# The first two token tiles of a feed-forward layer take their 16 hidden blocks in two alternating halves

## The chip, the cores and the metric

The kernel runs on one core of one Trainium2 chip. The metric is the device time of one execution in microseconds (us), the median of several runs. Beside it stands one profiled execution, from which all durations below come. Engines: PE is TensorE (matmul), DVE is VectorE, ACT is ScalarE, POOL is GpSimd, SP is SyncE, which here only issues DMAs.

## The reference, cut to what matters

A linear recurrence (state space attention) over 4 sequences of 768 steps with 8 heads is followed by a feed-forward layer over all 3072 tokens:

```python
# recurrence, chunk by chunk, for batch 4, heads 8, S = 768, D = 32, N = 16
L = np.exp(cum[:, :, :, None] - cum[:, :, None, :]) * causal
y_intra = np.einsum('bhij,bhjd->bhid', (Cc @ Bc.T) * L, xc)
y_inter = np.einsum('bhin,bhnd->bhid', Cc, state) * decay_to_i
state = decay_full * state + sum_j(Bc[j] * xc[j] * decay_from_j)
y[:, :, sl] = y_intra + y_inter
...
x = y.transpose(0, 2, 1, 3).reshape(3072, 256)
h = x @ w_in                       # w_in  [256, 2048]
g = softplus(h)
out = g @ w_out                    # w_out [2048, 256]
```

`w_in` and `w_out` arrive as float64. Every product of the feed-forward layer is done as three float32r matmuls of high and low parts, so the weights, the recurrence's output and the hidden values are all split in a high and a low part on the chip.

## The kernel before, in words

**Units and tiles.** The recurrence goes by 24 units of 128 tokens (`un0` to `un23`; 6 units to a sequence). The feed-forward layer goes by 6 token tiles of 512 tokens (`sizes`), so tile j needs units 4j to 4j+3. The hidden width of 2048 is cut into 16 blocks of 128 (`NFT`). A step (j, k) is block k of tile j.

**A step.** `first(j, k)` makes the hidden block `hp` in one of six PSUM banks (tag `ps`) by 6 matmuls of 512 columns: `xh*wih`, `xl*wih`, `xh*wil` for two halves of the contraction. ACT then makes the softplus `e` (3 buffers) and its rounded copy `gh` (4 buffers), and DVE the rest `gl = e - gh` (L531). `second(j, k)` adds the block to the two accumulators `acc0` and `acc1` by 6 more matmuls; each accumulator has one PSUM bank (pool `pa`). `second` of step s is written LAG = 8 steps after `first` of step s. When the last block of a tile is added, `finish(j)` copies `acc0` by DVE and `acc1` by ACT and sends both out.

**A unit.** Its rows arrive in `un` (3 buffers). POOL makes the decay mask `rm` (2 buffers), PE the scores `sp`, DVE the masked scores `m` (two instructions), PE the state update `zp` and the output `yp`, DVE the new `state` and the output `y`; ACT rounds `y` into the tile's `xh`, and POOL or DVE makes `xl = y - xh` (DVE for units 2, 4 and 7). Units from 8 on also need two DVE instructions on their raw B and C rows (`b_rows`, `c_all`, L199), and `c_all` is copied by DMA into `c_rows`, of which there is one. The first four units are written out by hand in the word list `ORDER`.

**The weights.** Sixteen loads `wraw0` to `wraw15` (even numbers: 2 blocks of `w_in`; odd: 2 blocks of `w_out`) each go through ACT (L475), three DVE instructions (L477, L479, L481), ACT (L484, the high part) and POOL or DVE (L486, the low part).

**What sets the order.** From step 0 on the program is written step by step: each step's `first`, softplus and split, the `second` of eight steps earlier, and then what is planned in that step: a unit's parts (`LATE`, `V_LAG`), loads, and one weight split a step in the order `W_ORDER`. A scheduler then puts each engine's instructions in one fixed order by its own estimate of times; on the chip each engine works its list in order, and an instruction that waits holds up all behind it on that engine.

Of the kernel before, what the change touches and what calls it, by code (L numbers as in the profile page):

```python
# [10 lines left out]
F32 = mybir.dt.float32  # L11
F32R = mybir.dt.float32r
I32 = mybir.dt.int32
BF16 = mybir.dt.bfloat16
AF = mybir.ActivationFunctionType
ALU = mybir.AluOpType
PSUM = bass.MemoryType.PSUM

P = 128
# [7 lines left out]
NFT = DFF // P  # L27
TOK = NB * S
HEAD = 4
# [22 lines left out]
ORDER = """  # L52
# [2 lines left out]
C3 I1 G0 G1 S3 warm1 R2 gg4 M2 W2 I2 R3 warm1 W0 X1 zero M3 w6 W2 I3 W2 G3 W2 X0 w4 X3 G2 w3 un5 X2  # L55
H0 H1
"""
W_ORDER = (0, 1, 4, 3, 2, 6, 10, 8, 5, 7, 12, 9, 14, 11, 13, 15)
LAG = 8
LATE = (1, 1, 1, 1, -1, -2, -1, -1)  # L60
V_LAG = (0, 0, 1, 0, 0, 2, 0, 0)

V_BP = (0, 2, 7)
V_CC = (0, 1, 2, 6, 7)
# [32 lines left out]
def recurrence_then_ffn(ctx: ExitStack, tc: tile.TileContext, fst, un, at, al, w_in, w_out, const, outT):  # L97
# [6 lines left out]
    p3 = ctx.enter_context(tc.tile_pool(name="p3", bufs=3))  # L104
# [17 lines left out]
    V, A, Pl, PE = (InOrder(e) for e in (nc.vector, nc.scalar, nc.gpsimd, nc.tensor))  # L122
# [3 lines left out]
    def load(out, in_):  # L126

        tc.keep_in_program_order(nc.sync.dma_start(out, in_))  # L128
# [143 lines left out]
    sizes = [512] * 6  # L272
    starts = [sum(sizes[:j]) for j in range(len(sizes))]
    xparts = {}

    def x_parts(t0):
        j = max(i for i in range(len(sizes)) if starts[i] <= t0)
        if j not in xparts:
            xparts[j] = [p3.tile([P, 2, 512], F32R, tag=f"x{v}", name=f"x{v}_{j}", bufs=2) for v in "hl"]
        return xparts[j], t0 - starts[j]  # L280

    bd = kb[:, 0 : NH // 2]
# [132 lines left out]
    def grow(i):  # L415
        y = mid[i]["y"] = p2.tile([P, 2, P], F32, tag="y", name=f"y{i}")
        V.tensor_tensor(y, mid[i]["yp"][:, : 2 * P].rearrange("p (g t) -> p g t", g=2), gg_s[i], op=ALU.mult)
        (xh, xl), c0 = x_parts(i * P)
        A.copy(xh[:, :, c0 : c0 + P], y)  # L419

    def rest(i):
        (xh, xl), c0 = x_parts(i * P)
        hi = xh[:, :, c0 : c0 + P].bitcast(F32)
        (V if i in V_XL else Pl).tensor_tensor(xl[:, :, c0 : c0 + P], mid.pop(i)["y"], hi, op=ALU.subtract)  # L424
# [19 lines left out]
    raws = {}  # L444

    def load_w(step):
        raw = p3.tile([P, 512, 2], I32, tag="wraw", name=f"wraw{step}", bufs=6)
        q = step // 2
        if step % 2 == 0:
            load(  # L450
                raw.rearrange("p (c f) t -> p c (f t)", c=2),
                w_in.rearrange("(c p) f -> p c f", p=P)[:, :, 512 * q : 512 * q + 512],
            )
        else:
            load(
                raw.rearrange("p (k e) t -> p k (e t)", k=2),
                w_out.rearrange("(k p) e -> p k e", p=P)[:, 2 * q : 2 * q + 2, :],
            )
        raws[step] = raw
# [33 lines left out]
    accs, parts = {}, {}  # L493
# [3 lines left out]
    def products(j, k, h, c0, c1):  # L497
        xh, xl = x_parts(starts[j])[0]
        fs = slice(k * P, (k + 1) * P)
        i = 0  # L500
        for c in range(2):
            for w, x in ((wih, xh), (wih, xl), (wil, xh)):
                PE.matmul(h[:, c0:c1], w[:, c, fs], x[:, c, c0:c1], start=i == 0, stop=i == 5)  # L503
                i += 1
# [28 lines left out]

    def second(j, k):
        n = sizes[j]
        if k == 0:
            accs[j] = [pa.tile([P, 512], F32, tag=f"acc{e}", name=f"acc{e}_{j}") for e in range(2)]
        acc = accs[j]
        gh, gl = parts.pop((j, k))
        for e in range(2):  # L540
            es = slice(e * P, (e + 1) * P)
            for i, (w, g) in enumerate(((woh, gh), (woh, gl), (wol, gh))):
                PE.matmul(  # L543
                    acc[e][:, :n], w[:, k, es], g, start=k == 0 and i == 0, stop=k == NFT - 1 and i == 2
                )

    def finish(j):
        t0, n = starts[j], sizes[j]
        for e in range(2):
            o = p2.tile([P, 512], F32, tag=f"o{e}", name=f"o{e}_{j}", bufs=1)  # L550
            if e == 0:
                V.tensor_copy(o[:, :n], accs[j][e][:, :n])  # L552
            else:
                A.copy(o[:, :n], accs[j][e][:, :n])
            load(outT[e * P : (e + 1) * P, t0 : t0 + n], o[:, :n])
# [22 lines left out]
    stages = defaultdict(list)  # L578
# [6 lines left out]
    def both(f, i):  # L585
# [11 lines left out]
        "un": load_unit,  # L597
        "gg": load_growth,
        "w": load_w,
        "loga": lambda _: log_clipped(la),  # L600
        "logr": lambda _: log_clipped(lr),
# [18 lines left out]
    for word in ORDER.split():  # L620
        name = word.rstrip("0123456789")
        acts[name](int(word[len(name) :] or 0))
    steps = [(j, k) for j in range(len(sizes)) for k in range(NFT)]

    def values(s):
        if s >= LAG:
            j, k = steps[s - LAG]
            second(j, k)
            if k == NFT - 1:
                finish(j)  # L630

    in_order[0] = False

# [2 lines left out]
    def plan(s, f, *args):  # L636
        fills[s].append((f, args))

    for i in range(HEAD, NB * NU):
        s = (i - HEAD) * NFT // 4  # L640
        late, wait = (LATE[i - HEAD], V_LAG[i - HEAD]) if i - HEAD < len(LATE) else (0, 2)
        s += late
        plan(s, prepare, i)
        plan(s, attend_scores, i)
        plan(s + wait, attend_values, i)
        if i + 2 < NB * NU:
            plan(s + 1, prefetch, i + 2)
    loads = [w for w in W_ORDER if f"w{w}" not in ORDER.split()]
    splits = [w for w in W_ORDER if w not in stages]
    for s, w in enumerate(splits):  # L650
        plan(s, split_w, w)
    for s, w in enumerate(loads):
        plan(s, load_w, w)
    for s in range(len(steps) + LAG):
        if s < len(steps):
            first(*steps[s])
            soft_part(*steps[s])
            split_part(*steps[s])
        values(s)
        for f, args in fills[s]:  # L660
            f(*args)
# [50 lines left out]
```

## Time and profile before

| What | Value |
|---|---|
| Median of 3 runs | 356.2 us (354.79 to 357.56) |
| The profiled execution: its time | 354.56 us |
| Its span, first to last instruction | 352.6 us |
| Busy over the span: PE, DVE, ACT, POOL | 94%, 56%, 48%, 32% |
| DVE busy per 10 us, from 40 to 100 us | 9.97, 9.89, 7.83, 9.23, 10.00, 10.00 us |
| DVE busy per 10 us, from 110 to 150 us | 4.14, 5.94, 5.08, 5.87 us |
| Mean granted TensorE clock | 0.98 |

PE's busy share says little by itself, since matmuls overlap and the end of each is modelled. How fast PE really moves is read from the starts of its matmuls, or from the chain of waits, which counts six 512-column matmuls as 1.36 us. The feed-forward layer alone is 96 x 12 = 1152 of them.

### The profile page before, as it was taken

To read this page: it belongs to the slowest core of one execution; us is meant where nothing else is said; L and a number is where in the kernel's file an instruction comes from. 1 tells how busy PE (TensorE), PEld (TensorE's weight loads), DVE (VectorE), ACT (ScalarE), POOL (GpSimd) and SP (SyncE) were. 2 spreads that over 40 slices of the span, in tenths; PEclk is the share of its full clock that TensorE was granted. 3 is DMA by queue.
4 is the path that set the end of the run, shared out by engine and by line. 5 is a ranking of instruction groups with operands and counts; after the bars stand their busy time and mean duration, and the time that the engine had idled before them with its cause. 6 is when DMAs were issued, how large, how long until landed. Compare 5 with 4: busy or idle time off the path is not lost.

```text
span 352.6 us, 5070 instructions
## 1 busy us (share of the span) xinstructions
PE 332.8 (94%) x1882; PEld 252.0 (71%) x1882; DVE 196.0 (56%) x300; ACT 168.4 (48%) x297; POOL 114.0 (32%) x142
## 2 busy tenths in 40 slices
PE   6878985999999999999999999999999999999995
PEld 3533653567677877787877787787787788888884
DVE  1676999799984545553653553754363523132231
ACT  2311835584665535454644544645353534344450
POOL 6576943557631125323143322323512000000000
PEclk9689999899999999999999999999999999999999
DMA  7889745364210752141543222552303100001001
GB/s 203 222 196 335 252 136 187 120 257 144 51 70 8 214 152 91 30 135 48 162 121 109 65 82 71 140 161 93 91 30 89 31 2 0 0 23 40 0 2 59
DMA packets 22264, 37.23 MB, mean 106 GB/s; under 512 B 1632, under 2 KB 12896, under 8 KB 22240
## 3 DMA queue, kind: packets, MB, share of 16 engines
q1 hardware_dynamic: 22240, 36.91, 34.6%
q8 instruction: 15, 0.25, 0.3%
q14 instruction: 9, 0.07, 0.1%
HBM read 29.46 MB, written 3.24 MB: 93 GB/s over the span
## 4 chain that ended last, share of the span: by engine, by line
PE 76%; DMA 9%; DVE 8%; issue 2%; SPq 2%; ACT 1%; DVEq 0%; ACTq 0%
PE acc L543 33%; PE hp L503 32%; DMA wraw<-in_w_out 3%; DMA gg<-gd 3%; PE yp L407 3%; DVE w L479 2%; PE yp L393 2%; PE sp L339 2%; SPq L128 2%; DMA head_c<-in_fst 2%; DVE gl L531 1%; DMA c_rows<-c_all 1%; DVE w L477 1%; DVE w L481 1%; PE zp L364 1%
## 5 line engine op out<-in xcount | busy, mean ns | idle before, releaser
L531 DVE TENSOR_TENSOR gl<-e,gh 128x512 fp32r<-128x512 f32 x96 | 71.5, 746 | 83.0 <-ACT gh L530 82.3
L530 ACT CAST gh<-e 128x512 fp32r<-128x512 f32 x96 | 59.3, 620 | 65.2 <-PE acc L543 64.2
L503 PE MATMUL hp<-xh,wih 128*128 128x512 f32 (+1 forms) x192 | 77.2, 405 | 6.3 <-ACT wih L484 5.1
L523 ACT ACTIVATE e<-hp 128x512 f32<-128x512 f32 x96 | 56.6, 595 | 49.6 <-DVE gl L531 42.3
L543 PE MATMUL acc<-gl,woh 128*128 128x512 f32 x192 | 75.0, 390 | 0.0
L503 PE MATMUL hp<-xl,wih 128*128 128x512 f32 (+1 forms) x192 | 74.9, 391 | 0.0
L543 PE MATMUL acc<-gh,wol 128*128 128x512 f32 x192 | 74.9, 393 | 0.0
L503 PE MATMUL hp<-xh,wil 128*128 128x512 f32 (+1 forms) x192 | 74.3, 390 | 0.0
L543 PE MATMUL acc<-gh,woh 128*128 128x512 f32 x192 | 73.1, 392 | 0.2 <-DVE o L552 0.2
L503 PEld LDWEIGHTS hp<-xh,wih 128*128 128x128 f32 x192 | 36.1, 188 | 19.4 <-ACT wih L484 6.0
L292 POOL TENSOR_SCALAR_AFFINE_SELECT rm<-fc 128x1024 f32<-128x1024 f32 x20 | 32.1, 1605 | 47.8 <-DVE m L350 47.7
L543 PEld LDWEIGHTS acc<-gh,woh 128*128 128x128 f32 x192 | 36.0, 188 | 8.2 <-issue 0.8
L503 PEld LDWEIGHTS hp<-xh,wil 128*128 128x128 f32 x192 | 36.1, 188 | 8.0 <-issue 0.2
L543 PEld LDWEIGHTS acc<-gh,wol 128*128 128x128 f32 x192 | 36.0, 188 | 7.9 <-issue 0.2
L543 PEld LDWEIGHTS acc<-gl,woh 128*128 128x128 f32 x192 | 36.1, 188 | 7.5
L503 PEld LDWEIGHTS hp<-xl,wih 128*128 128x128 f32 x192 | 36.4, 189 | 6.5 <-issue 0.2
L350 DVE TENSOR_TENSOR m<-sp,rm 128x512 f32<-128x512 f32 x40 | 26.2, 684 | 14.0 <-PE sp L339 12.5
L199 DVE SCALAR_TENSOR_TENSOR c_all<-un,kb,c_all 128x512 fp32r<-128x512 f32 x16 | 17.3, 1084 | 10.4 <-ACT c_all L198 10.2
L424 POOL TENSOR_TENSOR xl<-y,xh 128x256 fp32r<-128x256 f32 x18 | 14.0, 780 | 25.8 <-ACT xh L419 25.2
L320 POOL TENSOR_TENSOR r_apart<-un,fr 64x128 f32<-64x128 f32 x32 | 17.1, 534 | 14.1 <-DMA un<-in_un 10.1
L307 POOL TENSOR_TENSOR bp<-un,ft 128x128 f32<-128x128 f32 x15 | 7.4, 491 | 42.1 <-DMA un<-in_un 23.7
L383 POOL TENSOR_TENSOR tb<-state,kb 128x128 f32<-128x128 f32 x16 | 11.9, 744 | 23.6 <-DVE state L375 23.0
(96 smaller groups left out, 306.5 us busy)
## 6 DMA issues: line engine op xcount, KB each, us to landing
un<-in_un SPq DMA_DIRECT2D x16, 768.0 KB, 4.5
wraw<-in_w_in SPq DMA_DIRECT2D x8, 512.0 KB, 7.8
wraw<-in_w_out SPq DMA_DIRECT2D x8, 512.0 KB
c_rows<-c_all SPq DMA_DIRECT2D x32, 128.0 KB, 2.4
gg<-gd SPq DMA_DIRECT2D x16, 192.0 KB
out_t<-o SPq DMA_DIRECT2D x12, 256.0 KB
un<-in_fst SPq DMA_DIRECT2D x4, 576.0 KB, 9.6
head_c<-in_fst SPq DMA_DIRECT2D x8, 128.0 KB, 6.5
```

The lines of the kernel that those rows point to most:

```text
L199: V.scalar_tensor_tensor(out, raw, g, out.bitcast(F32), op0=ALU.mult, op1=ALU.add)
L292: Pl.affine_select(out=rm.rearrange("p h c i -> p (h c) i"), in_=fc[:, u].rearrange("p h c -> p (h c)").unsqueeze(2).broadcast_to([P, NH * ...
L320: (V if i in V_CC else Pl).tensor_tensor(cc[rows, g], un_s[i][rows, U_C:U_S].rearrange("p (c i) -> p c i", i=SUB), f_row[b][rows, u, :NC]. ...
L350: V.tensor_tensor(mid[i]["m"][:, 4 * g : 4 * g + 4].rearrange("p h t -> p (h t)"), mid[i].pop(("sp", g)), mid[i]["rm"][:, 4 * g : 4 * g + ...
L383: (V if i in V_TB else Pl).tensor_tensor(tb, state[i - 1].rearrange("p (e d) -> p e d", d=D).unsqueeze(1).broadcast_to([P, 2, 2, D]), bd.r ...
L407: PE.matmul(yp[32 * hh : 32 * hh + 32, g * P : (g + 1) * P], un_s[i][:, U_X + h * D : U_X + (h + 1) * D], m[:, h, :], start=u == 0, stop=u ...
L424: (V if i in V_XL else Pl).tensor_tensor(xl[:, :, c0 : c0 + P], mid.pop(i)["y"], hi, op=ALU.subtract)
L503: PE.matmul(h[:, c0:c1], w[:, c, fs], x[:, c, c0:c1], start=i == 0, stop=i == 5)
L523: A.activation(e, h, AF.Softplus)
L530: A.copy(gh, e)
L531: V.tensor_tensor(gl, e, gh.bitcast(F32), op=ALU.subtract)
L543: PE.matmul(acc[e][:, :n], w[:, k, es], g, start=k == 0 and i == 0, stop=k == NFT - 1 and i == 2)
```

## The change

Tiles 0 and 1 take their 16 blocks in halves, alternating: blocks 0 to 7 of tile 0, blocks 0 to 7 of tile 1, blocks 8 to 15 of tile 0, blocks 8 to 15 of tile 1. From tile 2 on the order is as before. After each first half ACT copies both accumulators into a buffer in SBUF (`keep_sums`, in a slot of the tag `wraw`), and `finish` of these two tiles adds it to the second half's sums by two DVE instructions. So the second eight blocks' weights are first used at step 16 in place of step 8, and tile 1's tokens at step 8 in place of step 16: units 4 to 7 are planned at steps 0, 1, 3 and 5 (before: 1, 5, 9 and 13), units 8 to 11 at 12, 16, 20, 24 (before: 15, 18, 23, 27), and the weight splits by the table `W_STEP` over steps 0 to 24, each loaded eight steps ahead. The raw weights get 5 buffers in place of 6, the tiles' inputs `xh`, `xl` 3 in place of 2.

```diff
-W_ORDER = (0, 1, 4, 3, 2, 6, 10, 8, 5, 7, 12, 9, 14, 11, 13, 15)
+W_ORDER = (0, 2, 4, 1, 6, 3, 5, 7, 8, 10, 12, 14, 9, 11, 13, 15)
+W_STEP = (0, 0, 0, 1, 3, 5, 7, 9, 11, 13, 15, 16, 18, 20, 22, 24)
 LAG = 8
-LATE = (1, 1, 1, 1, -1, -2, -1, -1)
-V_LAG = (0, 0, 1, 0, 0, 2, 0, 0)
+HALF = NFT // 2
+U_STEP = (0, 1, 3, 5, 12, 16, 20, 24)
+V_LAG = (0, 1, 1, 1, 0, 1, 0, 0)
...
-            xparts[j] = [p3.tile([P, 2, 512], F32R, tag=f"x{v}", name=f"x{v}_{j}", bufs=2) for v in "hl"]
+            xparts[j] = [p3.tile([P, 2, 512], F32R, tag=f"x{v}", name=f"x{v}_{j}", bufs=3) for v in "hl"]
...
-        raw = p3.tile([P, 512, 2], I32, tag="wraw", name=f"wraw{step}", bufs=6)
+        raw = p3.tile([P, 512, 2], I32, tag="wraw", name=f"wraw{step}", bufs=5)
...
     def second(j, k):
         n = sizes[j]
-        if k == 0:
+        if k % HALF == 0 and (k == 0 or j < 2):
             accs[j] = [pa.tile([P, 512], F32, tag=f"acc{e}", name=f"acc{e}_{j}") for e in range(2)]
...
+    def keep_sums(j):
+        both = p3.tile([P, 512, 2], I32, tag="wraw", name=f"half_{j}", bufs=5)
+        for e in range(2):
+            t = sums_of[j, e] = both.rearrange("p f t -> p (f t)").bitcast(F32)[:, 512 * e : 512 * e + 512]
+            A.copy(t, accs[j][e])
...
     def finish(j):
...
-            if e == 0:
+            if j < 2:
+                V.tensor_tensor(o, accs[j][e], sums_of[j, e], op=ALU.add)
+            elif e == 0:
...
-    steps = [(j, k) for j in range(len(sizes)) for k in range(NFT)]
+    steps = [(j, k) for v in range(2) for j in range(2) for k in range(v * HALF, v * HALF + HALF)]
+    steps += [(j, k) for j in range(2, len(sizes)) for k in range(NFT)]
...
             if k == NFT - 1:
                 finish(j)
+            elif k == HALF - 1 and j < 2:
+                keep_sums(j)
...
-        s = (i - HEAD) * NFT // 4
-        late, wait = (LATE[i - HEAD], V_LAG[i - HEAD]) if i - HEAD < len(LATE) else (0, 2)
-        s += late
+        s, wait = (U_STEP[i - HEAD], V_LAG[i - HEAD]) if i - HEAD < len(U_STEP) else ((i - HEAD) * NFT // 4, 2)
...
-    for s, w in enumerate(splits):
-        plan(s, split_w, w)
-    for s, w in enumerate(loads):
-        plan(s, load_w, w)
+    for s, w in zip(W_STEP, W_ORDER):
+        if w not in stages:
+            plan(s, split_w, w)
+        if f"w{w}" not in ORDER.split():
+            plan(max(s - 8, 0), load_w, w)
```

Line numbers of the changed kernel are 3 higher than before's in the parts named here (L484 for L481, and so on), and 18 higher at the end. In the rows below names read tile, unit or block, and a running number: `hp0_12_770` is the hidden block 12 of tile 0, `gl0_5_586` the low part of block 5 of tile 0, `y7_643` the output of unit 7, `xl_1_428` the low input of tile 1, `acc0_0_687` the first accumulator of tile 0.

On DVE, around the last unit of tile 1, before:

```order
L481 SCALAR_TENSOR_TENSOR w11_763<-wraw11_625,w11_763 128x512
L479 SCALAR_TENSOR_TENSOR w13_789<-wraw13_655,w13_789 128x512
L417 TENSOR_TENSOR y7_847<-yp7_837,gg6_476 128x256
L481 SCALAR_TENSOR_TENSOR w13_789<-wraw13_655,w13_789 128x512
L486 TENSOR_TENSOR wol_88<-w11_763,woh_87 128x512
L424 TENSOR_TENSOR xl_1_449<-y7_847,xh_1_448 128x2x128
```

and now:

```order
L489 TENSOR_TENSOR wol_88<-w7_716,woh_87 128x512
L420 TENSOR_TENSOR y7_643<-yp7_633,gg6_454 128x256
L534 TENSOR_TENSOR gl0_6_621<-e0_6_618,gh0_6_620 128x512
L480 TENSOR_SCALAR w10_860<-w10_860 128x512
L534 TENSOR_TENSOR gl0_7_662<-e0_7_659,gh0_7_661 128x512
L482 SCALAR_TENSOR_TENSOR w10_860<-wraw10_609,w10_860 128x512
L427 TENSOR_TENSOR xl_1_428<-y7_643,xh_1_427 128x2x128
```

Unit 7's output stood behind the three integer steps of fourteen weights and 12 of tile 0's `gl`; now it stands behind those of nine weights and 6 `gl`. Its low part `xl_1` is DVE's 53rd instruction after the second `m` of unit 4, where it was the 72nd.

On PE, where block 7 of tile 0 is added, before:

```order
L543 MATMUL acc0_0_640<-gh0_7_614,woh_87 128x512
L543 MATMUL acc0_0_640<-gl0_7_615,woh_87 128x512
L543 MATMUL acc0_0_640<-gh0_7_614,wol_88 128x512
L543 MATMUL acc1_0_641<-gh0_7_614,woh_87 128x512
L543 MATMUL acc1_0_641<-gl0_7_615,woh_87 128x512
L543 MATMUL acc1_0_641<-gh0_7_614,wol_88 128x512
L543 MATMUL acc0_0_640<-gh0_8_636,woh_87 128x512
```

and now:

```order
L506 MATMUL hp1_3_744<-xh_1_427,wih_85 128x512
L506 MATMUL hp1_4_770<-xh_1_427,wih_85 128x512
L342 MATMUL sp8_0_799<-c_rows_81,b_rows8_789 128x256 x2
L546 MATMUL acc0_0_687<-gl0_7_662,woh_87 128x512
L546 MATMUL acc0_0_687<-gh0_7_661,wol_88 128x512
L546 MATMUL acc1_0_688<-gl0_7_662,woh_87 128x512
L546 MATMUL acc1_0_688<-gh0_7_661,wol_88 128x512
L506 MATMUL hp1_0_674<-xl_1_428,wih_85 128x512
L506 MATMUL hp1_0_674<-xh_1_427,wil_86 128x512
```

Block 8 of tile 0 followed on block 7; now the products of tile 1 follow, of which the first matmul of each of five blocks stands ahead, and all the others behind the one that needs `xl_1`.

More of the change, by code (lines that the diff above doesn't have):

```diff
@@ L543, in second @@
                 PE.matmul(
-                    acc[e][:, :n], w[:, k, es], g, start=k == 0 and i == 0, stop=k == NFT - 1 and i == 2
-                )
+                    acc[e][:, :n],
+                    w[:, k, es],
+                    g,
+                    start=i == 0 and (k == 0 or k == HALF and j < 2),
+                    stop=i == 2 and (k == NFT - 1 or k == HALF - 1 and j < 2),
+                )
+    sums_of = {}
+    def keep_sums(j):
[3 more added lines that the diff above has]
+            A.copy(t, accs[j][e])
     def finish(j):
@@ L647, in recurrence_then_ffn @@
             plan(s + 1, prefetch, i + 2)
-    loads = [w for w in W_ORDER if f"w{w}" not in ORDER.split()]
-    splits = [w for w in W_ORDER if w not in stages]
-    for s, w in enumerate(splits):
-        plan(s, split_w, w)
-    for s, w in enumerate(loads):
-        plan(s, load_w, w)
+    for s, w in zip(W_STEP, W_ORDER):
[3 more added lines that the diff above has]
+            plan(max(s - 8, 0), load_w, w)
     for s in range(len(steps) + LAG):
```

## The prediction

> **What bounds the kernel now.** I read the page's slices first, then the chain of waits, PE's and DVE's rows in order of time, and last the counts of matmuls by stage.
>
> ```profile
> span 352.6 us, 5070 instructions
> PE   6878985999999999999999999999999999999995
> DVE  1676999799984545553653553754363523132231
> PEclk9689999899999999999999999999999999999999
> ```
>
> A slice is 8.8 us. DVE is full from the fifth slice to the eleventh and half idle afterwards, when PE is full: up to about 100 us DVE sets the pace, then PE. The last stops of PE, in its rows by time:
>
> ```profile
> 61.31 0.50 PE L503 MATMUL hp<-xh,wih 128*128 128x512 f32 x1 [3.74 <-ACT wih L484]
> 90.31 0.67 PE L393 MATMUL yp<-r_apart,tb 128*128 128x256 f32 x2 [0.84 <-DVE y L417]
> 113.66 0.47 PE L543 MATMUL acc<-gh,woh 128*128 128x512 f32 x1 [0.20 <-DVE o L552]
> ```
>
> From 91 us on PE waits for next to nothing (0.2 us at the change of accumulators), so the change can only win or lose what PE stands idle before. How much is that? PE's matmuls that started between 35 and 105 us, one answer by stage for each of the tiles hp, acc, sp, yp, zp in this order (columns: stage, length, PE busy with count, clock, DMA share, GB/s), and the prices, from the chain (start, length, what) and from PE's rows:
>
> ```profile
> 35.00:105.00 70.00, 32.43 (x127) 0.98 0.47 155
> 35.00:105.00 70.00, 20.88 (x78) 0.98 0.47 155
> 35.00:105.00 70.00, 5.73 (x20) 0.98 0.47 155
> 35.00:105.00 70.00, 7.60 (x106) 0.98 0.47 155
> 35.00:105.00 70.00, 1.89 (x40) 0.98 0.47 155
> ```
> ```profile
> 108.03 1.36 PE hp L503 x6
> 98.19 0.60 PE sp L339 x4
> 104.49 0.57 PE yp L407 x16
> ```
> ```profile
> 43.69 1.13 PE L334 MATMUL sp<-un 64*128 64x512 f32 x4
> 120.22 0.32 PE L364 MATMUL zp<-un,bp 128*32 128x64 f32 x8
> 120.47 0.70 PE L393 MATMUL yp<-r_apart,tb 128*128 128x256 f32 x2
> 120.82 0.58 PE L503 MATMUL hp<-xh,wih 128*128 128x512 f32 x1
> ```
>
> A 512-column matmul costs 1.36/6 = 0.227 us; zp of a unit 0.25 and its first yp 0.35 (start to start). hp: 115 whole ones 26.1 and 12 of half the columns, at half the price, 1.4; acc: 78 x 0.227 = 17.7; sp: three units by L334 3 x 1.1 = 3.3 and eight by L339 1.2; yp: 96/16 x 0.57 = 3.4 and 10/2 x 0.35 = 1.8; zp: 40/8 x 0.25 = 1.3. Together 56.2 of 70 us: **PE loses 13.8 us there**, most of it in many short pieces. That is the ceiling of any gain.
>
> **The change part by part.** It adds no matmul. It asks for other things earlier: tile 1's inputs, which need units 4 to 7, stand before the second eight blocks' weights. DVE does both, so I follow its new order. Prices are DVE's groups between 37.6 and 91.6 us, while it is the bound (count, busy, mean ns, idle before):
>
> ```profile
> L531 DVE TENSOR_TENSOR gl<-e,gh 128x512 fp32r<-128x512 f32 x12 | 10.9, 912 | 0.8 <-ACT gh L530 0.8
> L479 DVE SCALAR_TENSOR_TENSOR w<-wraw,w 128x512 int32<-128x512 int32 x12 | 10.7, 896 | 0.1
> L481 DVE SCALAR_TENSOR_TENSOR w<-wraw,w 128x512 int32<-128x512 int32 x12 | 10.4, 869 | 0.1
> L477 DVE TENSOR_SCALAR w<-w 128x512 int32<-128x512 int32 x12 | 7.2, 609 | 0.7 <-ACT w L475 0.7
> L350 DVE TENSOR_TENSOR m<-sp,rm 128x512 f32<-128x512 f32 x7 | 4.7, 681 | 1.3 <-PE sp L334 1.3
> L199 DVE SCALAR_TENSOR_TENSOR b_rows<-un,kb,b_rows 128x512 fp32r<-128x512 f32 x2 | 3.5, 1758 | 0.0
> L199 DVE SCALAR_TENSOR_TENSOR c_all<-un,kb,c_all 128x512 fp32r<-128x512 f32 x2 | 2.3, 1168 | 0.0
> L424 DVE TENSOR_TENSOR xl<-y,xh 128x256 fp32r<-128x256 f32 x2 | 0.8, 412 | 0.0
> L375 DVE SCALAR_TENSOR_TENSOR state<-state,fr,zp 128x64 f32<-128x64 f32 x2 | 0.5, 268 | 0.0
> ```
>
> Busy times overlap a little at the joints. These rows make 51.0 us; six smaller groups of the same answer bring it to 55.8, while the 54.0 us hold 54.0 - 3.0 idle = 51.0: factor 0.915. A wol takes m's 0.68.
>
> *The start.* DVE and ACT rows of the head:
>
> ```profile
> 32.89 0.43 DVE L477 TENSOR_SCALAR w<-w 128x512 int32<-128x512 int32 x1 [2.47 <-ACT w L475]
> 37.61 0.68 DVE L350 TENSOR_TENSOR m<-sp,rm 128x512 f32<-128x512 f32 x1
> ```
> ```profile
> 36.35 0.68 ACT L475 ACTIVATE w<-wraw 128x512 f32<-128x512 f32 x1 [0.51 <-DMA wraw<-in_w_in]
> ```
>
> The first row is w1, whose three integer steps (0.61 + 0.90 + 0.87 = 2.4 us) now run in time when DVE is half waiting; in the new order they stand behind unit 4's scores. The third row is w4, at the same place of SP's list as before, so landing when it did: its L477 follows at 37.0, the second m of unit 4 at 37.4 (before 37.6), w1's L477 at 38.0. The 2.4 us thus move into the full stretch, and nothing before it gets shorter.
>
> *To xl_1.* From 38.4 us the new list has 52 instructions to unit 7's xl: 15 of L479/L481 at 0.88 = 13.2, 8 gl 7.3, 6 L477 3.7, 6 m 4.1, 2 b_rows 3.5, 2 c_all 2.3, 1 wol 0.7, 4 y and 2 xl at 0.41 = 2.5, 6 small ones at 0.27 = 1.6: 38.9 x 0.915 = 35.6. So xl_1 is done at 74.0, and y of unit 7, five instructions (3.4 us) earlier, at 70.6.
>
> *PE up to there.* PE's new list from 35 us to the matmul that needs xl_1: 41 of hp 9.3, the 12 half ones 1.4, 48 of acc 10.9, sp 3 x 1.1 + 0.3 = 3.6, zp 0.8, yp 4 x 0.57 + 3 x 0.35 = 3.3: 29.3 us. It is done early and waits: gl of block 6 is ready at 71.4, then 6 acc (1.4), 5 hp (1.1), sp (0.3), 4 acc (0.9): 75.1. Lost by then: 75.1 - 35 - 29.3 = 10.8 us.
>
> *After it.* The softplus has three buffers, so a bank of hp comes free only as DVE finishes a gl. With the same prices gl of blocks 0, 4 and 5 of tile 1 end at 83.7, 100.2 and 102.9, the scores of unit 9 at 96.8. PE, working on from 75.1, meets them 0.7 us early (block 6 of tile 1), 1.7 (unit 9's output), 1.7 (block 11 of tile 0) and 0.4 (block 12), each with about 0.6 us for the softplus: 4.5 us. Then the last split of a weight is past and PE has work to the end, as before.
>
> **The sum: 10.8 + 4.5 = 15.3 us lost against 13.8, +1.5 us**: from the profiled execution's 354.56 (its span 352.6 and 2.0 around it) to 356.1. The median of the three runs lies 1.6 above that execution; I forecast against the median: 356.2 + 1.5 = **357.7 us**.
>
> *The half sums* I cost at nothing. The copy's row of before:
>
> ```profile
> L554 ACT COPY o<-acc 128x512 f32<-128x512 f32 x6 | 3.5, 582 | 4.8 <-PE acc L543 4.8
> ```
>
> Two ACT copies take 1.2 us, two DVE adds 1.4 (as m, which also takes one side from PSUM). Between the last acc of one half and the first of the next PE's list holds 25, 24 and 6 hp matmuls, 5.7, 5.4 and 1.4 us, which cover them; bare, the four changes would cost 1.2 to 1.4 each, 5 us in all. On ACT the softplus of tile 1 stands behind the first copies, and waits until block 7 is added; that is in the 75.1. The fifth raw buffer: w3 now waits for w0's slot, whose last reader is long done.
>
> **The rivals.**
>
> *Faster.* The means above hold collisions with POOL:
>
> ```profile
> 38.86 1.74 POOL L292 TENSOR_SCALAR_AFFINE_SELECT rm<-fc 128x1024 f32<-128x1024 f32 x1
> 39.49 1.64 DVE L481 SCALAR_TENSOR_TENSOR w<-wraw,w 128x512 int32<-128x512 int32 x1
> 52.00 0.68 DVE L481 SCALAR_TENSOR_TENSOR w<-wraw,w 128x512 int32<-128x512 int32 x1
> 95.09 0.88 DVE L199 SCALAR_TENSOR_TENSOR b_rows<-un,kb,b_rows 128x512 fp32r<-128x512 f32 x1
> ```
>
> An L481 that starts while POOL works ends half a microsecond after POOL's and takes 1.64, alone 0.68; b_rows alone 0.88. Over the 52 instructions the excess is 15 x 0.20 + 8 x 0.23 + 2 x 0.88 = 6.6 us. If the new order meets POOL half as often, 3.3 us go by xl_1 and some 2 of the 4.5 behind it: 352.5. For it: collisions are a matter of phase, and the order is new. Against: POOL's list holds as many masks and low parts per microsecond. It decides if unit 7's y ends before 67. The Trainium skill ("SBUF — State Buffer", Who interferes with whom) has VectorE instructions with two SBUF inputs and GpSimd's reads share a port that whoever starts first keeps; the rows at 38.86 and 39.49 agree. By that rule alone the price stays as long as both lists hold the same instructions.
>
> *Slower.* Units 6 to 8 must arrive within a few microseconds of each other, and DVE's list now holds an instruction of unit 7 (bp) due at 50 us, with all behind it waiting. SP issues un7 behind wraw7, whose buffer comes free at about 42.
>
> ```profile
> 53.21 0.41 SPq L128 DMA_DIRECT2D un<-in_fst  x1
> 59.10 0.29 DVE L307 TENSOR_TENSOR bp<-un,ft 128x128 f32<-128x128 f32 x1
> ```
> ```profile
> un<-in_fst SPq DMA_DIRECT2D x4, 576.0 KB, 9.6
> ```
>
> Un7 now took at most 5.9 us, but the median of its kind is 9.6: 42.5 + 9.6 = 52, a stall of 2 us; the same again for un8 and un10 makes 4. Then PE's waits before 75 us are long ones, and the one of 3.74 us at 61.31 was followed by
>
> ```profile
> 62.80 2.08 PE L334 MATMUL sp<-un 64*128 64x512 f32 x4
> ```
>
> where 1.13 is usual, in the slice whose clock reads 8: 1 to 2 us more. That gives 357.7 + 4 + 1.5 = 363. The point from which it decides: un7 later than 50 us. The Trainium skill ("TensorE: Matmul & The Clock Gate", Why this matters for your kernels) warns of PE gaps over about 3 us, after which the clock halves; the row at 62.80 agrees, and by it a halved clock at 75 us would cost these 1 to 2 us even without late loads.
>
> *The half sums lie bare* after all: 5 us, 362.7.
>
> **How the numbers follow.** I give the forecast 0.42 (its own range 355 to 361), the faster rival 0.27, the slower one 0.26, the bare half sums 0.05. About 1%, 3.6 us, is what a measurement tells from no change. Faster by over 1%: 0.22 of the faster rival and 0.02 of the forecast, 0.24. Slower: 0.24 of the slower rival, 0.04 of the bare sums and 0.06 of the forecast, 0.34. Same: 0.42. The range 351.5 to 363 goes from just under the faster rival to the slower one.
>
> **What would show it.** In the changed kernel's profile: DVE without idle from 38 to 100 us; xl of unit 7 at 74 us (67 to 70 for the faster rival, 78 for the slower); PE's last long wait near 100 us in place of 90; bp of unit 7 near 50 us without a wait for un; no wait over 0.3 us of acc for o or for the half sums. The forecast is wrong if PE's loss between 35 and 105 us, counted as above, is under 10 or over 19 us.

## The result and the profile after

Over 20 runs each, taken in turn on the same chips, the changed kernel's median is 357.5 us (356.55 to 360.15) and that of the kernel before 356.25 us (354.25 to 357.56). The ratio is 1.0058, with a 95% interval of 1.0040 to 1.0076: a little slower, some 2 us, and within the 1% that the prediction called no change. The forecast was 357.7. Slow executions, among them one of combo2 with 1,820 us and one of combo2_wlv with 378 us, stand in no ratio below.

The changed kernel's page, the rows that answer to those shown of before:

```profile
span 356.2 us, 5076 instructions
PE   8969787899989999999999999999999999999995
DVE  1575899999997442566554544663463433132231
PEclk9987999699999999999999999999999999999999
```

The span is 3.6 us longer than before's 352.6, more than the medians differ; why single executions scatter like this is told below. DVE is full one slice longer, to the twelfth. PE has new dents in the fifth slice and in the eighth, where the granted clock reads 6; the dent in the seventh is shallower than before.

PE's rows in order of time, the longer waits from 60 us on and what stands behind the first of them:

```profile
63.37 0.50 PE L506 MATMUL hp<-xh,wih 128*128 128x512 f32 x1 [2.52 <-DVE y L420]
65.33 0.65 PE L410 MATMUL yp<-m,un 128*32 128x128 f32 x8 [0.52 <-DVE m L353]
70.80 0.63 PE L546 MATMUL acc<-gh,woh 128*128 128x512 f32 x1
71.23 0.63 PE L546 MATMUL acc<-gl,woh 128*128 128x512 f32 x1
72.06 0.40 PE L546 MATMUL acc<-gh,woh 128*128 128x512 f32 x1
72.29 0.39 PE L546 MATMUL acc<-gl,woh 128*128 128x512 f32 x1
79.16 0.39 PE L506 MATMUL hp<-xl,wih 128*128 128x512 f32 x1
100.02 0.67 PE L396 MATMUL yp<-r_apart,tb 128*128 128x256 f32 x2 [0.58 <-DVE m L353]
104.09 0.51 PE L506 MATMUL hp<-xh,wih 128*128 128x512 f32 x1 [0.98 <-ACT e L526]
```

PE's last wait has gone from 90.31 to 104.09 us. Between 66 and 72 us the matmuls start 0.43 us apart, afterwards 0.23. The row at 79.16 is the first matmul that needs the xl of unit 7.

DVE's rows, between the end of the head and that xl:

```profile
37.56 0.43 DVE L480 TENSOR_SCALAR w<-w 128x512 int32<-128x512 int32 x1 [1.44 <-ACT w L478]
37.90 0.68 DVE L353 TENSOR_TENSOR m<-sp,rm 128x512 f32<-128x512 f32 x1
38.84 1.75 DVE L482 SCALAR_TENSOR_TENSOR w<-wraw,w 128x512 int32<-128x512 int32 x1
46.15 1.75 DVE L534 TENSOR_TENSOR gl<-e,gh 128x512 fp32r<-128x512 f32 x1
47.82 1.51 DVE L480 TENSOR_SCALAR w<-w 128x512 int32<-128x512 int32 x1
52.38 1.38 DVE L310 TENSOR_TENSOR bp<-un,ft 128x128 f32<-128x128 f32 x1
73.18 0.41 DVE L420 TENSOR_TENSOR y<-yp,gg 128x256 f32<-128x256 f32 x1
76.76 0.41 DVE L427 TENSOR_TENSOR xl<-y,xh 128x256 fp32r<-128x256 f32 x1
```

No row between 37.90 and 80 us shows an idle time. The y of unit 7 ends at 73.6 (predicted 70.6) and its xl at 77.2 (74.0).

PE's matmuls that ran between 35 and 105 us, one answer by stage for each of hp, acc, sp, yp, zp, as for the kernel before:

```profile
35.00:105.00 70.00, 29.93 (x118) 0.95 0.55 174
35.00:105.00 70.00, 20.82 (x68) 0.95 0.55 174
35.00:105.00 70.00, 5.14 (x22) 0.95 0.55 174
35.00:105.00 70.00, 8.49 (x106) 0.95 0.55 174
35.00:105.00 70.00, 1.59 (x40) 0.95 0.55 174
```

Two of the 22 sp matmuls were only running at 35 us; they started at 34.73, so 20 count. With the prediction's prices: hp 106 x 0.227 + 12 half ones 1.4 = 25.5, acc 15.4, sp 12 x 0.275 + 8 x 0.15 = 4.5, yp 5.2, zp 1.3, together 51.9. **PE loses 18.1 us of the 70, against 13.8 before: 4.3 us more, where the two spans differ by 3.6.** By the matmul at 79.16 it has lost 79.16 - 35 - 29.3 = 14.9, and behind it 3.2.

### The profile page after: what moved, and what is told of

It is laid out like the page before. It is cut to its first block, busy times and chain, and to the rows that moved or that the text cites. A ratio compares the mean times of both kernels' runs of the same rounds, so it can differ in the third digit from the quotient of the medians.

```text
span 356.2 us, 5076 instructions
## 1 busy us (share of the span) xinstructions
PE 338.6 (95%) x1882; PEld 254.3 (71%) x1882; DVE 200.5 (56%) x302; ACT 169.6 (48%) x299; POOL 114.7 (32%) x142
## 4 chain that ended last, share of the span: by engine, by line
PE 72%; DVE 13%; DMA 7%; issue 3%; ACT 2%; POOL 0%; SPq 0%; DVEq 0%; ACTq 0%
PE acc L546 32%; PE hp L506 31%; DMA wraw<-in_w_in 5%; DVE w L482 3%; DVE w L484 3%; DVE w L480 2%; PE yp L410 2%; DVE gl L534 2%; PE yp L396 2%; DMA gg<-gd 2%; PE sp L342 2%; PE fp L122 1%; PE sp L122 1%; DVE m L353 1%; DMA la<-in_at 1%
## 5 line engine op out<-in xcount | busy, mean ns | idle before, releaser
L534 DVE TENSOR_TENSOR gl<-e,gh 128x512 fp32r<-128x512 f32 x96 | 75.8, 790 | 83.4 <-ACT gh L533 82.7
L546 PE MATMUL acc<-gl,woh 128*128 128x512 f32 x192 | 75.8, 395 | 0.0
L546 PE MATMUL acc<-gh,woh 128*128 128x512 f32 x192 | 74.5, 399 | 0.0
L506 PEld LDWEIGHTS hp<-xh,wih 128*128 128x128 f32 x192 | 36.0, 188 | 16.7 <-issue 3.6
L353 DVE TENSOR_TENSOR m<-sp,rm 128x512 f32<-128x512 f32 x40 | 26.3, 685 | 13.6 <-PE sp L342 13.1
L202 DVE SCALAR_TENSOR_TENSOR c_all<-un,kb,c_all 128x512 fp32r<-128x512 f32 x16 | 14.9, 932 | 9.6 <-ACT c_all L201 9.5
L410 PE MATMUL yp<-m,un 128*32 128x128 f32 x320 | 14.3, 286 | 4.1 <-DVE m L353 2.4
```

Of the source, the lines that this page charges most:

```text
L202: V.scalar_tensor_tensor(out, raw, g, out.bitcast(F32), op0=ALU.mult, op1=ALU.add)
L353: V.tensor_tensor(mid[i]["m"][:, 4 * g : 4 * g + 4].rearrange("p h t -> p (h t)"), mid[i].pop(("sp", g)), mid[i]["rm"][:, 4 * g : 4 * g + ...
L410: PE.matmul(yp[32 * hh : 32 * hh + 32, g * P : (g + 1) * P], un_s[i][:, U_X + h * D : U_X + (h + 1) * D], m[:, h, :], start=u == 0, stop=u ...
L534: V.tensor_tensor(gl, e, gh.bitcast(F32), op=ALU.subtract)
L546: PE.matmul(acc[e][:, :n], w[:, k, es], g, start=i == 0 and (k == 0 or k == HALF and j < 2), stop=i == 2 and (k == NFT - 1 or k == HALF - ...
```

## The experiments

The theory was that DVE's list sets the time up to PE's last wait, and with it what PE loses. The rivals: the low granted clock between 65 and 72 us is the loss; the half sums are; how often DVE's rows meet POOL's is what the two orders differ in. All ratios are against the kernel before, timed on the same chip. For "PE's loss" the matmuls of each profile that start from 35 us to the time that heads the column were counted one by one, at the prices above without rounding; by this count before has 14.0 at 105 us and the changed kernel 18.3.

| kernel | ratio (95%) | loss by 80 | by 105 | by 125 us |
|---|---|---|---|---|
| before | 1 | 11.2 | 14.0 | 14.9 |
| changed | 1.0058 (1.0040 to 1.0076) | 14.9 | 18.3 | 18.8 |
| no_half | 1.0072 (1.0045 to 1.0100) | 15.7 | 18.1 | 19.5 |
| clock6 | 1.0117 (1.0080 to 1.0153) | 12.7 | 16.7 | 17.6, and 2.1 of extra work |
| w1_first | 1.0026 (0.9999 to 1.0052) | 13.1 | 16.3 | 16.8 |
| u_late | 1.0025 (0.9997 to 1.0053) | 14.9 | 15.4 | 16.5 |
| pf_late | 1.0089 (1.0055 to 1.0123) | 12.1 | 19.3 | 19.8 |
| u_late_pf | 1.0086 (1.0057 to 1.0114) | 11.4 | 17.4 | 18.0 |
| combo2, again as combo2b | 0.9963 (0.9938 to 0.9988), 0.9983 (0.9955 to 1.0011) | 13.0 | 13.7 | 14.7 |
| wlv | 1.0021 (1.0000 to 1.0043) | 14.7 | 16.5 | 16.7 |
| before_wlv | 0.9929 (0.9905 to 0.9954) | 9.9 | 11.5 | 12.3 |
| combo2_wlv | 0.9906 (0.9871 to 0.9942) | 10.2 | 11.3 | 12.1 |
| combo_wlv | 0.9862 (0.9819 to 0.9904) | 9.1 | 10.2 | 10.7 |

A kernel with a smaller loss is the faster one almost throughout. The losses are of one execution each, so a microsecond between two of them says little. The row of combo2 has the losses of combo2b's profile. Where the expectations name 19.4 for the changed kernel's loss by 125 us, this count gives 18.8.

**The half sums (no_half).** This kernel leaves out the copies of the first halves and the adds, so its outputs of tiles 0 and 1 hold the second eight blocks alone. The edit in short:

```diff
 def keep_sums(j):
-        both = p3.tile([P, 512, 2], I32, tag="wraw", ...)
-        for e in range(2): ... A.copy(t, accs[j][e])
+        return
 def finish(j):
-            if j < 2: V.tensor_tensor(o, accs[j][e], sums_of[j, e], op=ALU.add)
-            elif e == 0:
+            if e == 0:
```

> The two copies of each half sum and the two adds are left out (the output of tiles 0 and 1 then holds the second eight blocks alone; their first half is computed and thrown away). Theory (covered by hp matmuls): ratio stays within 0.002 of the changed kernel's 1.006. Rival (the half sums are what the change costs): 1.2 to 5 us come back, ratio 0.992 to 1.002.

1.0072, no gain: the half sums cost nothing that can be measured. DVE's list is the changed kernel's up to the adds, so this profile is also a repeat of it. Two of its DVE rows and PE's waits:

```profile
39.49 0.43 DVE L480 TENSOR_SCALAR w<-w 128x512 int32<-128x512 int32 x1 [0.54 <-ACT w L478]
78.70 0.41 DVE L427 TENSOR_TENSOR xl<-y,xh 128x256 fp32r<-128x256 f32 x1
```
```profile
65.33 0.50 PE L506 MATMUL hp<-xh,wih 128*128 128x512 f32 x1 [2.52 <-DVE y L420]
77.29 0.50 PE L546 MATMUL acc<-gl,woh 128*128 128x512 f32 x1 [1.56 <-DVE gl L534]
```

From the L480 of w4 to the xl of unit 7 it takes 78.70 - 39.49 = 39.21 us; in the changed kernel 76.76 - 37.56 = 39.20. The head before it ended 1.9 us later, and the span is 358.2 instead of 356.2. So the full stretch of DVE repeats to a hundredth of a microsecond, and what scatters from one execution to the next is the head, where ACT waits for the transfer of a weight (3.38 us in no_half, 2.27 in the changed kernel).

**The granted clock (clock6).** Six redundant pairs of matmuls fill the gap at 60.9 us (the edit in short):

```diff
 def read(i):
+        for _ in range(6 if i == 7 else 0):
+            PE.matmul(yp[:, : 2 * P], tb, cc, start=True, stop=True)
```

> Six extra, redundant 256-column matmul pairs (0.35 us each, 2.1 us) stand in PE's list just ahead of the first output matmul of unit 7, in the gap of 2.5 us at 60.9 us after which the granted clock was low; the scheduler moves three rows of DVE's list behind xl of unit 7 for it. Both theories: if the gap is what lowers the clock, the acc matmuls between 65 and 73 us are 0.23 apart and not 0.43. Theory (DVE sets the end of the catch-up at 104 us): PE only waits longer at 77 to 104 us, ratio 1.004 to 1.007. Rival (the low clock is the loss): 2 us come back, ratio 1.000.

The granted clock of the two kernels, in the stage from 60 to 70 us (PE, PEld, DVE, ACT and POOL busy, then clock, DMA share, GB/s), first the changed kernel, then clock6:

```profile
60.00:70.00 10.00, 6.87 (x32) 3.93 (x32) 10.00 (x14) 6.07 (x12) 8.87 (x8) 0.76 0.58 145
```
```profile
60.00:70.00 10.00, 7.50 (x44) 5.42 (x44) 10.00 (x14) 6.07 (x12) 8.82 (x9) 1.00 0.54 149
```

Filling the gap kept the clock at 1.00, and PE reached its first matmul with the xl of unit 7 at 76.09 us, three microseconds sooner. Not all of that is the clock's doing, since the scheduler also moved three DVE rows behind this xl, which ends at 75.9 instead of 77.2. Nothing of it arrived at the end: PE then waited more often up to 103 us, and with the 2.1 us of extra work the loss is 19.7 against 18.8. The time is 1.0117, no gain and rather slower; that it lies above both expectations is not explained. A pair of profiles with DVE's list unchanged says the same. Between 65 and 75 us, where the clock is low, the changed kernel loses 3.8 us and the kernel before 1.0. But in no_half the low clock lasted for 3.4 us and in the changed kernel for 6.8; in no_half PE stood 1.56 us for a gl instead (the row at 77.29), and by 105 us the two have lost 18.1 and 18.3. In these profiles the low clock is mostly another way of waiting for DVE. The Trainium skill ("TensorE: Matmul & The Clock Gate", Why this matters for your kernels) warns of gaps over about 3 us; here 2.52 us were enough.

**The two ends of DVE's list (w1_first, u_late, combo2).**

```diff
-W_ORDER = (0, 2, 4, 1, 6, 3, 5, 7, 8, 10, 12, 14, 9, 11, 13, 15)
+W_ORDER = (0, 2, 1, 4, 6, 3, 5, 7, 8, 10, 12, 14, 9, 11, 13, 15)   # w1_first, combo2
-U_STEP = (0, 1, 3, 5, 12, 16, 20, 24)
+U_STEP = (0, 1, 3, 5, 16, 20, 24, 28)                               # u_late, combo2
```

> Only the order of two early weight splits goes back: w1 stands ahead of w4 again, so its three integer steps are done while DVE is still half waiting. Theory (DVE's full stretch sets the time): xl of unit 7 ends about 2 us earlier, at 75 instead of 77.1 us, and PE is dense from about 102 instead of 104 us; ratio to the kernel before 1.000 instead of 1.006. Rival (the low granted clock of 65 to 72 us is what costs the time): no change unless that clock stays up; ratio 1.005. Rival (half sums bare): no change, 1.006.

> Only four numbers change: units 8 to 11 are planned at steps 16, 20, 24, 28 instead of 12, 16, 20, 24. DVE's list is word for word the same up to xl of unit 7 and three rows on; then the weights and the gl of tile 1 stand ahead of the scores and row splits of units 8 to 10. Theory (DVE's list sets PE's waits after 79 us too): the waits of PE at 100 and 104 us go, about 2 us of the 3.7 lost by the profile come back, ratio 1.001. Rival (all of the loss is before 79 us, by the late xl and the low clock): nothing comes back, 1.005.

> The two order edits together: w1 split ahead of w4, and units 8 to 11 planned at steps 16, 20, 24, 28. Each alone stood at 1.0026 and 1.0025. Theory (both take DVE work off the stretch before PE's last wait, the one at its start, the other at its end): the gains add, ratio 0.999. Rival (both win back the same wait at 100 to 104 us): 1.002.

> The two order edits together once more, for a profile of an undisturbed execution: ratio 0.996 as before; PE's last wait over 0.4 us before 80 us, and its loss between 35 and 125 us about 4 us under the changed kernel's 19.4.

w1_first: 1.0026, half of what was expected. DVE's rows, two of w1's steps, the second m of unit 4 and the xl of unit 7:

```profile
35.46 0.68 DVE L482 SCALAR_TENSOR_TENSOR w<-wraw,w 128x512 int32<-128x512 int32 x1
37.21 0.68 DVE L484 SCALAR_TENSOR_TENSOR w<-wraw,w 128x512 int32<-128x512 int32 x1
39.50 0.68 DVE L353 TENSOR_TENSOR m<-sp,rm 128x512 f32<-128x512 f32 x1
77.28 0.41 DVE L427 TENSOR_TENSOR xl<-y,xh 128x256 fp32r<-128x256 f32 x1
```

The steps of w1 do run in the head, but from the m to the xl it takes 37.8 us instead of 38.9, only 1.1 less. The scheduler orders the list anew and put one step of another weight there, so 52 rows stand in place of 54, and they meet POOL at other places: the L484 steps take 2.9 us more, the gl 2.1 less.

u_late: 1.0025, near the 1.001 expected. DVE's list is the same up to the xl of unit 7, with 14.9 us lost by 80 us in both; behind it the changed kernel loses 3.4 more by 105 us, u_late 0.5, and no wait of PE over 0.4 us is left there. So what stands on DVE behind that xl also counted. The intervals of w1_first and u_late, each taken alone, still overlap the changed kernel's.

combo2: the gains at least add: 0.9963 and 0.9983, both clear of the changed kernel's interval, and the loss by 125 us is 14.7, before's 14.9. Both edits bring back a piece of the old order: w1 stood ahead of w4 there too, and units 8 to 11 were planned nearly as late. **The order in halves with two lines of its tables altered is no slower than the kernel before**, and probably a little faster.

**What stands ahead of the xl of unit 7 (pf_late, u_late_pf).**

```diff
-            plan(s + 1, prefetch, i + 2)
+            plan(s + 1 + {6: 6, 7: 6, 8: 2}.get(i, 0), prefetch, i + 2)
```

u_late_pf has the U_STEP of u_late beside it.

> The changed kernel with units 8, 9 and 10 loaded six, six and two steps later, so that the row splits of unit 9 (c_all, b_rows) and the last two gl of tile 0's first half stand behind xl of unit 7 on DVE, five rows fewer ahead of it (some 3.5 us); the same rows stand ahead of tile 1's fifth gl as before. Theory A (the list up to PE's last wait sets the time, here to 104 us): xl of unit 7 ends near 73.5 instead of 77.1, the waits at 100 and 104 us grow or stay, ratio 1.004 to 1.006. Theory B (what PE loses before xl of unit 7 is what the change costs): 2 to 3 us come back, ratio 0.998 to 1.000.

> The same later loads together with units 8 to 11 planned four steps later (alone 1.0025, PE with no wait over 0.4 us after 66). Theory A: the last wait now lies before xl of unit 7, so what stands ahead of it counts: 2 us more come back, ratio 0.997. Theory B: the gain is the sum too, 0.996 to 0.998. If the row splits only wait somewhere else: 1.0025.

Rows of pf_late on DVE and PE, and one of u_late_pf on PE:

```profile
73.20 0.41 DVE L427 TENSOR_TENSOR xl<-y,xh 128x256 fp32r<-128x256 f32 x1
```
```profile
81.73 0.84 PE L342 MATMUL sp<-c_rows,b_rows 128*128 128x256 f32 x4 [2.06 <-DMA c_rows<-c_all]
```
```profile
91.95 0.32 PE L367 MATMUL zp<-un,bp 128*32 128x64 f32 x8 [3.63 <-ACT e L526]
```

In pf_late the xl starts at 73.2, as expected, and PE has lost 12.1 by 80 us instead of 14.9. Theory B then expected a faster kernel; it is 1.0089. The 3 us are given back within 10 us: the rows of unit 8 now reach PE late, through a transfer of c_rows that took up to 10.0 us to land (its median is 2.4), and the clock falls again behind that gap; by 105 us the loss is 19.3, the changed kernel's 18.3. That fits theory A, although the time lies a little above its range; but the late transfer is a cost of the edit itself, so the two theories are not cleanly parted here. For u_late_pf the forecasts of both theories failed altogether: 1.0086 instead of about 0.997. There DVE waits 1.25 us for a weight that ACT converts late (L478), and a gl behind it holds up the softplus, and PE with it, for 3.63 us. This edit costs as much as the shorter list wins.

**Collisions (wlv, before_wlv, combo2_wlv, combo_wlv).**

```diff
-WL_V = (2, 7, 10, 11, 15)
+WL_V = tuple(range(16))
```

wlv has this in the changed kernel, before_wlv in the one before; combo2_wlv has combo2's two edits beside it, and combo_wlv the later loads of pf_late as well.

POOL's rows beside the DVE rows at 46.15 and 47.82 in the changed kernel:

```profile
45.97 1.40 POOL L295 TENSOR_SCALAR_AFFINE_SELECT rm<-fc 128x1024 f32<-128x1024 f32 x1 [0.41 <-DVE m L353]
47.34 1.71 POOL L489 TENSOR_TENSOR wol<-w,woh 128x512 fp32r<-128x512 f32 x1
```

A gl that takes 0.68 alone takes 1.75 beside the first, and the shift of 0.43 takes 1.51 beside the second. The scores m, with one side from PSUM, never do:

```profile
L353 DVE TENSOR_TENSOR m<-sp,rm x40: 677/682/693, 35.4 to 288.9; 128x512 f32<-128x512 f32 x40
```

The Trainium skill ("SBUF — State Buffer", Who interferes with whom) says just this, that a VectorE instruction with at most one SBUF input, outside certain modes, doesn't contend with GpSimd; the trace agrees. Added up between 37.9 and 104 us, DVE's rows hold some 17.3 us over their undisturbed durations (the excess) in the changed kernel and 14.5 in the one before, of which 8.7 and 5.5 lie beside POOL's ten low parts. In no_half it is 17.2, so this too repeats. With the shortest row of each kind as the undisturbed one the sums come out about 1 us higher.

> The changed kernel, but every weight's low part (128x512 subtraction) is made by DVE, none by POOL. Between 37.9 and 104 us DVE's rows hold 17.3 us more than their undisturbed durations, 8.7 of it under POOL's ten low parts (the kernel before: 14.5 and 5.5). Theory (how often DVE's rows meet POOL's is what the two orders differ in): the 8.7 go, ten low parts of 0.60 us are added, so DVE is 2.7 us sooner through the same work and 2 us come back: ratio 1.000; no row of DVE stands over 1 us beside a low part. Rival (DVE's added 6 us count in full, POOL's work is free): ratio 1.013 or more. Rival (not DVE but the order itself): 1.006.

> The same edit in the kernel before: all low parts on DVE. Theory (collisions): 5.5 us go and 6.0 are added, so its time stays, ratio 0.998 to 1.002, and against it the changed kernel with the same edit is within 0.003, where the two without it differ by 0.006. Rival (the two orders differ for another reason): their difference stays 0.006.

> All three edits: low parts on DVE, w1 ahead of w4, units 8 to 11 four steps later. Theory: 2.7 us less on DVE beside the two order edits, ratio 0.994. Rival (DVE's added work counts in full): 1.006 or more.

> All four edits: low parts on DVE, w1 split ahead of w4, units 8 to 11 planned later, units 8 to 10 loaded later. Without the last it stood at 0.9906, and PE's rows held no wait over 0.4 us after 36 us. Theory: PE is the bound from 50 us on, so a shorter list ahead of xl of unit 7 is worth nothing more: 0.989 to 0.992. Rival (DVE still sets it): 0.986.

DVE is given eleven instructions more, ten of them in this stretch, and both kernels get faster: 1.0058 to 1.0021, and 1 to 0.9929. The excess falls to 10.0 and 8.3 us. In the changed kernel a low part thus costs DVE more on POOL (8.7 / 10 = 0.87 us) than on DVE itself (0.60), and the gain of 1.3 us is what this account gives (7.3 less excess, 6.0 more work). In the kernel before the account comes out even (5.5 / 10 = 0.55 against 0.60) and no gain was expected; why it gained 2.5 us all the same is not shown. What is refuted is the other half: the two orders should then have come within 0.003 of each other, and they stand 0.0092 apart. Collisions are a price that both pay; they are not what separates them. The two order edits are: with them (combo2_wlv, 0.9906) the order in halves is again no slower than before_wlv. PE's rows of wlv and of before_wlv say where the rest lies:

```profile
69.46 0.50 PE L546 MATMUL acc<-gh,woh 128*128 128x512 f32 x1 [2.79 <-ACT woh L487]
71.45 2.50 PE L506 MATMUL hp<-xh,wih 128*128 128x512 f32 x5 [0.79 <-ACT xh L422]
```
```profile
61.33 0.50 PE L503 MATMUL hp<-xh,wih 128*128 128x512 f32 x1 [2.72 <-ACT wih L484]
```

In wlv PE stands 2.79 us for a weight of tile 0's first half. DVE's rows show what its last step (L484) stood behind:

```profile
60.15 0.88 DVE L202 SCALAR_TENSOR_TENSOR b_rows<-un,kb,b_rows 128x512 fp32r<-128x512 f32 x1
67.06 0.89 DVE L202 SCALAR_TENSOR_TENSOR c_all<-un,kb,c_all 128x512 fp32r<-128x512 f32 x1
67.87 0.88 DVE L484 SCALAR_TENSOR_TENSOR w<-wraw,w 128x512 int32<-128x512 int32 x1
```

The first two are row splits (the DVE instructions on a unit's raw B and C rows) of units 8 and 9. Behind the gap PE runs at 0.50 us a matmul; by 80 us it has lost 14.7, before_wlv 9.9. Behind 73 us neither waits over 0.4 us any more. So here the low clock does seem to cost, since no later wait for DVE could hide it.

With all order edits the best is combo_wlv: 350.67 us against 355.0, **0.9862 (0.9819 to 0.9904), faster than both kernels**. Its only wait of PE over 0.4 us between 36 and 125 us is the first one:

```profile
37.98 0.70 PE L396 MATMUL yp<-r_apart,tb 128*128 128x256 f32 x2 [1.36 <-POOL r_apart L323]
```

Whether the later loads still add to combo2_wlv can't be told: 0.9906 and 0.9862 have overlapping intervals, and the losses of 12.1 and 10.7 leave room for it. The result stands at the rival's 0.986, and its interval reaches into the theory's range.

## Why the prediction was right, and where its steps were not

- **The outline held.** PE's last wait moved from 90 to 104 us (predicted: near 100), DVE stayed full (idle rows up to 100 us: 0.30 at 88 and 0.74 at 97), the half sums were covered, and the change only altered what PE loses before. Expected were 1.5 us more; the medians differ by 1.25, the ratio means 2.1, the two profiles 3.6.
- **"To xl_1" was too short.** The list was the predicted one, but took 38.3 us from 38.84 instead of 35.6, and began 0.4 later. DVE's groups between 38.7 and 77.0 us, to be set beside the prediction's:

```profile
L534 DVE TENSOR_TENSOR gl<-e,gh 128x512 fp32r<-128x512 f32 x8 | 9.3, 1167 | 0.0
L480 DVE TENSOR_SCALAR w<-w 128x512 int32<-128x512 int32 x7 | 5.5, 787 | 0.0
L202 DVE SCALAR_TENSOR_TENSOR b_rows<-un,kb,b_rows 128x512 fp32r<-128x512 f32 x2 | 2.6, 1318 | 0.0
L202 DVE SCALAR_TENSOR_TENSOR c_all<-un,kb,c_all 128x512 fp32r<-128x512 f32 x2 | 1.8, 885 | 0.0
```

The eight gl took 9.3 us instead of the 7.3 priced, the six L477 steps (now L480; the first of the seven, 0.41, began before) 5.1 instead of 3.7, bp 1.38 instead of 0.27 (its row at 52.38); b_rows and c_all were 1.4 cheaper. The factor 0.915 held (the rows add up to 42.0 us and took 38.3); what was too small is the sum of the prices, 38.9. They were means of the kernel before, with its collisions, and were taken for constants. The new order met POOL more: the rival that halved the collisions had the right mechanism with the wrong sign.
- **"PE up to there"** was therefore 10.8 on record and 14.9 in the trace.
- **"After it"** was 4.5 on record and 3.2 in the trace: of four waits two came, 0.58 and 0.98 us long, and not 1.7 each. The two errors, +4.1 and -1.3, partly cancel. The sum 15.3 met 18.1, inside the bounds of 10 and 19 that were set for it, but near the upper one.
- **The start.** The move of w1 was priced at 2.4 us in the full stretch. Undone alone, it is worth 0.3%, 1.1 us: one other step moved up, and the collisions fell elsewhere.
- **The slower rival's condition did not occur, one of its prices did.** The bp of unit 7 started at 52.38 without waiting for its unit. The low clock came nevertheless, behind a gap of 2.52 us. As far as clock6 and no_half show, it cost nothing at the end, because PE had to wait for DVE up to 104 us anyhow.
- **Right in the median, by some luck.** The profiled execution shows an added loss more than twice the forecast's. One pair of executions carries the scatter of two heads, up to 2 us here, so neither 3.6 nor 1.25 should be read to half a microsecond.

What stays open: which of the rows that now stand ahead of the xl of unit 7 makes up the 3.7 us by 80 us. Taking rows out made the scheduler put others there, in every kernel but u_late and no_half, so a single row's price could not be measured; only the sum of the order edits was. The buffers, five raw weights in place of six and three input tiles in place of two, were not tried apart from the order either.

## What to carry to other kernels

While one engine is full, shortening the list ahead of one result pays only if no later wait stands on the same list: look for the last wait, not the longest. An engine that looks free may be the dearer place for an operation if its accesses hold up the full one, as in the changed kernel; add up the excess of the full engine's rows over their undisturbed durations before offloading. A new order should be judged after its tables are tuned: here the same order in halves stood at 1.006 as it came and at 0.997 with two lines altered.

## What the hardware showed beyond that

- A stretch of 54 instructions with some 12 us of collisions in it repeated within 0.03 us: 39.20, 39.21 and, in u_late, 39.23 us. Collisions belong to the order of the lists and are no noise; the head's transfers are the noise.
- The granted clock fell to half after gaps of 2.52 us, in stretches that began about one to two microseconds after PE was at work again and lasted 6.8 us in one execution and 3.4 in another of the same list. Here are the changed kernel's stages of 2 us behind the gap that ended at 63.37 (PE busy, clock, DMA share, GB/s):

```profile
64.00:66.00 2.00, 1.48 (x13) 0.80 0.72 165
66.00:68.00 2.00, 2.00 (x11) 0.50 0.30 105
70.00:72.00 2.00, 2.00 (x6) 0.50 0.86 296
72.00:74.00 2.00, 2.00 (x10) 1.00 0.45 109
```

- The length of the gap does not decide alone: the one of 2.72 us in before_wlv was followed by no low clock at all, the one of 2.06 us in pf_late by a clock of 0.54 in the next two microseconds. One of 1.97 us in combo2b was followed by none, but in combo2_wlv the clock read 0.50 from 38 to 40 us behind a gap of only 1.37 us, and in wlv from 58 to 60 us behind one of 0.54. So no length of gap that would be safe can be read from these runs.
